# A new order of all steps in a causal-attention and SoLU feed-forward kernel

## The chip, the cores and the metric

One Trainium2 chip, one core of it. The metric is the device time of one execution in microseconds (us); the kernel before was timed three times, and one more execution was profiled. The core has TensorE (PE; its weight loads are PEld), VectorE (DVE), ScalarE (ACT), GpSimd (POOL), and SyncE (SP), which issues most DMA transfers. Each runs its instructions in the order in which they stand in its own queue.

## The reference

Eight batches of eight heads with 576 tokens of 64 numbers each. Four heads see the last 32 positions, four see every 32nd position before them. The attention output of all heads (4,608 tokens of 512 numbers) goes through a feed-forward layer of 1,024 with a SoLU activation and a normalisation.

```python
scores = scale * np.matmul(q, k.transpose(0, 1, 3, 2))
mask_local = (rel >= 0) & (rel < stride)
mask_strided = (rel >= 0) & (pos[None, :] % stride == pos[:, None] % stride)
...
attn = attn / (np.sum(attn, axis=-1, keepdims=True) + 1e-09)
return np.matmul(attn, v).astype(np.float32)
...
h = x @ w_in
h_max = np.max(h, axis=-1, keepdims=True)
e = np.exp(h - h_max)
sm = e / (np.sum(e, axis=-1, keepdims=True) + 1e-09)
solu = h * sm
mu = np.mean(solu, axis=-1, keepdims=True)
var = np.mean((solu - mu) ** 2, axis=-1, keepdims=True)
ln = (solu - mu) / np.sqrt(var + 1e-06) * g_ln
return (ln @ w_out).astype(np.float32)
```

## The kernel before, in words

**Two kinds of work.** Attention is cut into 34 units, each a run of query blocks of one batch and one kind of mask. A unit's steps, in turn: scores and mask on TensorE (L439, its products in L443 and L448), the rows' maximum (L454) and difference (L455) on VectorE, the exponential on ScalarE (L456), the sum (L457) and its reciprocal (L460) on VectorE, the scaling by it on GpSimd (L465), the upper half in 16 bits on ScalarE (L475), the lower half (L479 on VectorE; L477 on GpSimd for the first two batches), a transposing DMA (L481), the output products on TensorE (L487, L505), and a copy of them from PSUM by ScalarE (L543). Queries, keys and values of a batch are loaded by SyncE (L259); values are scaled and split in two 16-bit halves by ScalarE (L400) and VectorE (L401).

The feed-forward layer has 36 tiles of 128 tokens. Ten are plain (L603): two steps of twelve products each. The others go two by two (L646) in seven products of six matrix instructions each (L678, at L681 to L683), which take sums of tokens and of weights in place of some products; GpSimd forms the sums of tokens (L658), ScalarE and VectorE split them in halves (L667, L668), and VectorE joins the products (L706, L710), with a copy by ScalarE (L714). What follows for every tile (L726): the exponential (L746), the product with it (L749), the mean (L752), the centred value's two halves (L753 on ScalarE, L754 on VectorE), the sum of squares (L756), five small steps of GpSimd for the factor of the normalisation (L760 to L764), a transposing DMA (L767), the output product in two halves of twelve matrix instructions (L776, at L771 to L773), and the scaled store (L779). The weights come as 64-bit numbers and are decoded at the start by ScalarE and VectorE (L836 to L838).

**The order.** The function lists 1,598 steps in a `Plan`; a step has an engine, a function that issues its instructions, and the tiles that it reads and writes. Its number is its place of listing. They are issued in the order of the list `ORDER`, written out in the file; `order` only checks that it is complete and that each step stands behind those that it depends on. An engine's queue is thus the steps of that engine, in the order of the list:

```python
def order(self):
    place = {n: i for i, n in enumerate(ORDER)}
    assert sorted(ORDER) == list(range(len(self.steps)))
    assert all(place[d] < place[n] for n, s in enumerate(self.steps) for d in s[2])
    return ORDER
...
for n in plan.order():
    eng = plan.steps[n][0]
    k = len(nc.cur_bb.bb.instructions)
    plan.steps[n][1]()
```

Steps that the texts name by number: 749 and 940 are L754 of two tiles; 786, 788, 793 and 795 join products (L706, L710) and 787, 791, 794, 961, 965 are such products (L678); 628 and 807 are second halves of output products (L776); 848, 867 are scalings of attention units (L465); 1018 is the output product of a unit (L487); 1240, 1252, 1271 and 1292 are scores of four units of one batch (L439), whose output products are 1250, 1262, 1281 and 1302; 1087 to 1151 lie in the products of two pairs.

Of the kernel before, what the change touches and what calls it, by code (L numbers as in the profile page):

```python
# [56 lines left out]
    0, 12, 7, 9, 13, 14, 11, 18, 4, 2, 15, 19, 1, 124, 10, 17, 3, 58, 20, 67, 23, 59, 16, 68, 69, 60, 70, 61, 62, 63, 71, 80, 141, 93, 72, 81, 21, 27, 65, 82,  # L57
    94, 83, 66, 24, 31, 98, 84, 157, 8, 73, 85, 99, 25, 74, 100, 26, 28, 101, 111, 156, 102, 22, 35, 36, 29, 32, 33, 112, 75, 30, 34, 103, 113, 142, 37, 5,
    76, 158, 38, 39, 104, 40, 159, 96, 86, 41, 160, 161, 95, 42, 114, 162, 105, 259, 115, 56, 87, 258, 163, 165, 77, 88, 43, 97, 166, 116, 49, 44, 129, 167,
    57, 106, 293, 164, 168, 78, 89, 54, 266, 130, 169, 117, 45, 118, 267, 170, 268, 79, 47, 279, 131, 64, 292, 171, 46, 119, 125, 90, 143, 269, 50, 280, 52,  # L60
    91, 48, 55, 281, 282, 107, 260, 92, 270, 172, 120, 299, 108, 133, 300, 271, 51, 173, 53, 261, 121, 174, 109, 126, 144, 122, 127, 110, 195, 283, 272, 145,
    301, 132, 137, 262, 128, 325, 284, 175, 194, 134, 123, 146, 135, 294, 312, 147, 176, 138, 136, 295, 273, 274, 148, 196, 177, 197, 326, 313, 198, 210, 139,
    199, 302, 314, 200, 303, 264, 285, 263, 6, 265, 315, 201, 286, 316, 304, 275, 317, 140, 211, 327, 212, 226, 328, 329, 202, 213, 330, 215, 318, 203, 331,
    149, 305, 334, 214, 150, 216, 151, 335, 276, 306, 152, 204, 227, 430, 153, 336, 154, 277, 287, 278, 337, 338, 319, 242, 155, 228, 229, 339, 429, 178, 307,
    288, 308, 298, 180, 231, 297, 217, 289, 340, 296, 230, 290, 320, 179, 341, 232, 206, 181, 347, 233, 437, 220, 438, 342, 321, 291, 218, 439, 243, 309, 184,
    182, 310, 185, 183, 188, 311, 186, 348, 449, 189, 192, 207, 187, 193, 322, 190, 234, 191, 343, 244, 462, 245, 450, 332, 246, 208, 461, 247, 219, 440, 349,
    451, 431, 205, 248, 441, 502, 452, 344, 644, 468, 350, 501, 249, 503, 506, 453, 235, 209, 236, 432, 507, 504, 222, 351, 221, 352, 365, 345, 505, 469, 354,
    508, 510, 250, 353, 223, 442, 454, 511, 509, 252, 355, 512, 253, 470, 443, 251, 356, 366, 323, 346, 238, 471, 513, 436, 224, 514, 324, 367, 455, 368, 463,
    515, 444, 433, 516, 434, 370, 254, 357, 445, 381, 369, 519, 435, 371, 382, 456, 225, 237, 517, 472, 464, 457, 359, 383, 518, 520, 372, 239, 384, 397, 386,
    358, 521, 373, 524, 446, 465, 385, 467, 387, 398, 473, 361, 480, 388, 374, 399, 375, 400, 401, 389, 522, 240, 523, 525, 402, 403, 404, 481, 474, 241, 475,  # L70
    476, 390, 458, 407, 482, 413, 333, 414, 483, 377, 528, 415, 484, 447, 391, 255, 643, 448, 360, 405, 485, 459, 486, 477, 526, 466, 376, 416, 417, 527, 487,
    489, 490, 645, 256, 529, 491, 532, 651, 530, 676, 492, 257, 646, 493, 460, 652, 531, 675, 362, 653, 478, 418, 479, 408, 494, 654, 419, 363, 541, 533, 650,
    663, 655, 534, 542, 537, 538, 495, 649, 364, 406, 549, 656, 378, 535, 496, 657, 664, 539, 497, 543, 540, 420, 553, 536, 544, 550, 665, 545, 546, 551, 648,
    658, 488, 822, 666, 682, 659, 667, 379, 498, 547, 423, 683, 548, 499, 552, 393, 694, 668, 421, 392, 380, 684, 554, 422, 500, 685, 669, 555, 559, 557, 590,
    660, 591, 424, 594, 556, 598, 562, 558, 561, 677, 593, 596, 563, 577, 579, 599, 592, 560, 578, 409, 670, 678, 394, 425, 595, 580, 581, 564, 647, 671, 597,
    565, 695, 604, 582, 602, 583, 606, 686, 584, 600, 566, 395, 687, 567, 568, 601, 603, 605, 607, 608, 612, 569, 679, 571, 688, 570, 609, 615, 614, 616, 396,
    410, 630, 610, 672, 661, 631, 689, 632, 411, 586, 823, 633, 572, 634, 637, 680, 690, 696, 697, 662, 698, 699, 700, 681, 673, 412, 703, 701, 635, 704, 426,
    691, 611, 705, 830, 706, 824, 613, 674, 427, 707, 708, 825, 573, 831, 617, 709, 619, 855, 832, 692, 428, 693, 618, 720, 722, 842, 721, 718, 574, 833, 728,
    854, 715, 620, 710, 716, 636, 834, 717, 719, 621, 723, 843, 844, 827, 575, 724, 1000, 835, 732, 622, 711, 729, 725, 845, 730, 731, 624, 576, 587, 733,
    861, 826, 726, 862, 863, 836, 588, 623, 727, 625, 736, 837, 712, 773, 585, 713, 734, 589, 838, 738, 735, 639, 774, 737, 740, 739, 741, 626, 829, 743, 781,  # L80
    742, 714, 769, 744, 839, 756, 856, 757, 1001, 857, 864, 771, 846, 770, 777, 745, 785, 828, 758, 759, 746, 760, 772, 898, 778, 779, 865, 763, 847, 873,
    627, 761, 860, 747, 783, 848, 762, 782, 780, 849, 628, 850, 784, 748, 874, 750, 787, 786, 866, 867, 791, 629, 851, 775, 638, 899, 749, 788, 793, 794, 795,
    840, 868, 809, 702, 811, 810, 640, 869, 776, 841, 812, 813, 751, 789, 816, 875, 641, 858, 852, 876, 790, 859, 870, 877, 765, 878, 853, 792, 879, 910, 752,
    880, 882, 796, 906, 883, 1033, 814, 797, 871, 872, 884, 815, 894, 1008, 642, 1009, 895, 798, 885, 1010, 753, 1020, 754, 896, 886, 881, 902, 1032, 764,
    1011, 1002, 887, 799, 818, 900, 755, 1012, 903, 1021, 800, 888, 1003, 951, 1013, 817, 1014, 901, 907, 1022, 889, 1023, 908, 897, 766, 801, 1039, 909, 890,
    1233, 767, 904, 1040, 1007, 1015, 905, 912, 952, 891, 1024, 1016, 914, 1041, 803, 911, 892, 768, 1025, 1005, 802, 913, 916, 805, 919, 915, 804, 1026, 959,
    893, 917, 947, 1034, 918, 921, 1042, 920, 1017, 934, 948, 922, 1027, 936, 935, 1028, 1043, 937, 963, 938, 955, 923, 956, 806, 924, 949, 1006, 941, 939,
# [21 lines left out]
    1518, 1536, 1395, 1519, 1396, 1504, 1539, 1407, 1541, 1505, 1520, 1537, 1521, 1408, 1538, 1540, 1508, 1580, 1542, 1544, 1506, 1507, 1549, 1510, 1581,  # L109
    1545, 1523, 1546, 1409, 1509, 1551, 1547, 1548, 1552, 1511, 1550, 1554, 1582, 1512, 1555, 1553, 1567, 1569, 1556, 1568, 1522, 1570, 1557, 1571, 1572,  # L110
    1558, 1573, 1583, 1559, 1560, 1574, 1513, 1584, 1524, 1585, 1586, 1587, 1588, 1576, 1589, 1590, 1525, 1526, 1575, 1561, 1592, 1593, 1577, 1591, 1563,
    1578, 1562, 1564, 1594, 1595, 1565, 1596, 1579, 1566, 1597,
]

BANKED = ("h", "x")
# [881 lines left out]
```

## Time and profile before

| | |
|---|---|
| median of three runs | 556.56 us (555.68 to 556.75) |
| the profiled execution | 555.32 us |
| its span, from the first to the last instruction | 553.4 us |
| granted TensorE clock, mean over the span | 0.969 |
| busy: TensorE, VectorE, ScalarE, GpSimd | 470.8, 419.1, 327.5, 246.7 us |

A share of busy time is a mean over stages with different limits. Idle time of an engine is put down to the instruction whose end released it. TensorE's instructions are pipelined, and their ends are modelled; the granted clock is given as a share of the full 2.4 GHz.

### The profile page before, as it was taken

To read this page: it belongs to the slowest core of one execution; us is meant where nothing else is said; L and a number is where in the kernel's file an instruction comes from. 1 tells how busy PE (TensorE), PEld (TensorE's weight loads), DVE (VectorE), ACT (ScalarE), POOL (GpSimd) and SP (SyncE) were. 2 spreads that over 40 slices of the span, in tenths; PEclk is the share of its full clock that TensorE was granted. 3 is DMA by queue.
4 is the path that set the end of the run, shared out by engine and by line. 5 is a ranking of instruction groups with operands and counts; after the bars stand their busy time and mean duration, and the time that the engine had idled before them with its cause. 6 is when DMAs were issued, how large, how long until landed. Compare 5 with 4: busy or idle time off the path is not lost.

```text
span 553.4 us, 11936 instructions
## 1 busy us (share of the span) xinstructions
PE 470.8 (85%) x4788; PEld 238.6 (43%) x4788; DVE 419.1 (76%) x803; ACT 327.5 (59%) x475; POOL 246.7 (45%) x332
## 2 busy tenths in 40 slices
PE   4378978899989699795899799999889969799996
PEld 3254554434544245342454245343355524344442
DVE  2999879999798947689589965969848985756730
ACT  1997687656865656455466565655666645627440
POOL 3263347998684404423257322647413631462220
PEclk9978999999999999899899999999899999899999
DMA  8999998859969947676596939588766867550471
GB/s 338 372 320 254 271 219 205 166 121 216 254 149 209 224 84 223 96 146 189 111 234 111 191 116 243 134 148 165 214 111 180 146 141 103 100 90 25 101 146 57
DMA packets 168214, 95.78 MB, mean 173 GB/s; under 512 B 138080, under 2 KB 154848, under 8 KB 167648
## 3 DMA queue, kind: packets, MB, share of 16 engines
q1 hardware_dynamic: 162688, 84.84, 69.1%
q10 hardware_dynamic: 5472, 10.20, 6.0%
q8 instruction: 37, 0.61, 0.5%
q14 instruction: 17, 0.14, 0.1%
HBM read 39.24 MB, written 9.44 MB: 88 GB/s over the span
## 4 chain that ended last, share of the span: by engine, by line
DVE 39%; PE 27%; DMA 10%; issue 10%; ACT 9%; POOL 2%; ACTq 0%; SPq 0%; DVEq 0%; POOLq 0%
DVE c L754 5%; DVE eu L749 5%; DMA pt<-p 4%; PE o_ps L771 4%; DVE eu L710 3%; PE o_ps L772 3%; PE o_ps L773 3%; PE h_ps L681 3%; PE h_ps L683 3%; PE h_ps L682 3%; DVE m L457 2%; DVE p L479 2%; DVE m L454 2%; PE x_ps L505 2%; DMA ct<-c 2%
## 5 line engine op out<-in xcount | busy, mean ns | idle before, releaser
L771 PE MATMUL o_ps<-obuf,ct 128*128 128x512 f16 x272 | 105.6, 388 | 9.7 <-ACT ob L779 8.3
L465 POOL TENSOR_TENSOR t<-t,m 128x648 f32<-128x648 f32 (+4 forms) x34 | 55.8, 1644 | 113.8 <-DVE m L462 72.5
L772 PE MATMUL o_ps<-obuf,ct 128*128 128x512 f16 x272 | 104.8, 385 | 0.0
L773 PE MATMUL o_ps<-obuf,ct 128*128 128x512 f16 x272 | 104.6, 385 | 0.0
L658 POOL TENSOR_TENSOR x<-x 128x256 f32<-128x256 f32 x52 | 46.8, 913 | 80.8 <-ACT x L543 79.9
L754 DVE SCALAR_TENSOR_TENSOR c<-eu,st,c 128x1024 f16<-128x1024 f32 x36 | 54.0, 1507 | 11.0 <-ACT c L753 11.0
L753 ACT ACTIVATE c<-eu,st 128x1024 f16<-128x1024 f32 x36 | 41.0, 1143 | 26.5 <-DVE st L752 20.1
L746 ACT ACTIVATE eu<-eu,st,vsc 128x1024 f32<-128x1024 f32 x23 | 28.5, 1237 | 46.8 <-DVE st L736 46.0
L756 ACT ACTIVATE eu<-eu,st 128x1024 bf16<-128x1024 f32 x36 | 41.1, 1142 | 14.5 <-DVE st L752 13.7
L772 PEld LDWEIGHTS <-ct 128*128 128x128 f16 x288 | 28.6, 99 | 40.8 <-issue 11.4
L448 PE MATMUL s_ps<-k,q 64*54 64x54 f32 (+1 forms) x1280 | 41.0, 273 | 3.9 <-DMA q<-qstr 1.6
L771 PEld LDWEIGHTS <-ct 128*128 128x128 f16 x288 | 28.5, 99 | 36.0 <-DMA ct<-c 2.5
L773 PEld LDWEIGHTS <-ct 128*128 128x128 f16 x288 | 28.6, 99 | 35.5 <-issue 2.7
L454 DVE TENSOR_REDUCE m<-s_ps 128x12 f32<-128x648 f32 (+4 forms) x34 | 29.3, 861 | 17.5 <-PE s_ps L448 17.5
L448 PEld LDWEIGHTS s_ps<-k,q 64*54 64x54 f32 (+1 forms) x1280 | 39.9, 199 | 5.0 <-DMA q<-qstr 2.1
L683 PE MATMUL h_ps<-room,obuf 128*128 128x512 f16 x78 | 31.5, 404 | 12.3 <-DVE obuf L668 12.1
L706 DVE TENSOR_TENSOR eu<-eu,h_ps 128x512 f32<-128x512 f32 x39 | 26.7, 683 | 20.2 <-PE h_ps L683 18.4
L681 PE MATMUL h_ps<-room,obuf 128*128 128x512 f16 x78 | 31.4, 403 | 8.3 <-ACT eu L714 5.0
L749 DVE SCALAR_TENSOR_TENSOR eu<-eu,st 128x1024 f32<-128x1024 f32 x26 | 33.3, 1287 | 6.5 <-ACT eu L746 6.4
L779 ACT ACTIVATE ob<-o_ps,st 128x512 f32<-128x512 f32 x34 | 23.0, 677 | 21.4 <-PE o_ps L773 18.8
L456 ACT ACTIVATE t<-t 128x648 f32<-128x648 f32 (+4 forms) x34 | 26.1, 772 | 15.4 <-DVE t L455 14.8
L457 DVE TENSOR_REDUCE m<-t 128x12 f32<-128x648 f32 (+4 forms) x34 | 29.2, 860 | 4.3 <-ACT t L456 4.3
(207 smaller groups left out, 1101.6 us busy)
## 6 DMA issues: line engine op xcount, KB each, us to landing
out<-ob ACTq DMA_DIRECT2D x36, 256.0 KB, 3.4
vtwo<-vstr SPq DMA_DIRECT2D x8, 768.0 KB, 6.8
vd<-vtwo SPq DMA_DIRECT2D x14, 384.0 KB, 5.4
vrl<-vloc SPq DMA_DIRECT2D x8, 640.0 KB, 6.5
k<-kstr SPq DMA_DIRECT2D x8, 594.0 KB, 5.6
k<-kloc SPq DMA_DIRECT2D x8, 576.0 KB, 5.5
q<-qloc SPq DMA_DIRECT2D x8, 576.0 KB, 6.2
q<-qstr SPq DMA_DIRECT2D x7, 594.0 KB, 6.0
```

The lines of the kernel that those rows point to most:

```text
L448: nc.tensor.matmul(s_ps[row : row + nq, pair, i * nk : (i + 1) * nk], q_raw[half][hs, q0 : q0 + (nq - 1) * nqb + 1 : nqb], k_raw[half][hs, ...
L465: add("pool", lambda: nc.gpsimd.tensor_tensor(tv, tv, sm.unsqueeze(2).broadcast_to([P, nx, nk]), op=ALU.mult), r=TM, w=T)
L658: add("pool", lambda: nc.gpsimd.tensor_tensor(s[i], x, y, op=op), r=r, w=SS[i])
L681: nc.tensor.matmul(h_ps[:, bank], hi, w[0][:, c], start=(c == 0), stop=False)
L683: nc.tensor.matmul(h_ps[:, bank], lo, w[0][:, c], start=False, stop=(c == 1))
L749: add("dve", lambda: nc.vector.scalar_tensor_tensor(uv, hv, ia, ev, op0=ALU.mult, op1=ALU.mult, accum_out=us), r=[*HH, E, (ST, "ia")], w=[ ...
L753: add("act", lambda: nc.scalar.activation(c[:, 0], u, AF.Identity, bias=mean, scale=1.0), r=[*U, (ST, "mean")], w=[(C, 0)])
L754: add("dve", lambda: nc.vector.scalar_tensor_tensor(c[:, 1], u, mean, c[:, 0], op0=ALU.add, op1=ALU.subtract), r=[*U, (ST, "mean"), (C, 0) ...
L756: add("act", lambda: nc.scalar.activation(e.bitcast(BF16)[:, 0:DF], u, AF.Square, bias=mean, scale=1.0, accum_out=sq), r=[*U, (ST, "mean") ...
L771: nc.tensor.matmul(o, ct[:, cc, :], ohi[:, cc, :], start=(cc == 0), stop=False)
L772: nc.tensor.matmul(o, ct[:, cc, :], olo[:, cc, :], start=False, stop=False)
L773: nc.tensor.matmul(o, ct[:, 8 + cc, :], ohi[:, cc, :], start=False, stop=(cc == 7))
```

## The change

The list `ORDER` is replaced by another permutation of the same 1,598 numbers, with two-operand steps of VectorE and steps of GpSimd kept apart and idle stretches of TensorE kept short. Nothing else differs. Cut to the lines that hold the first and last steps and those named above:

```diff
--- before.py
+++ after.py
@@ -54,62 +54,62 @@
 
 
 ORDER = [
-    0, 12, 7, 9, 13, 14, 11, 18, 4, 2, 15, 19, 1, 124, 10, 17, 3, 58, 20, 67, 23, 59, 16, 68, 69, 60, 70, 61, 62, 63, 71, 80, 141, 93, 72, 81, 21, 27, 65, 82,
-    94, 83, 66, 24, 31, 98, 84, 157, 8, 73, 85, 99, 25, 74, 100, 26, 28, 101, 111, 156, 102, 22, 35, 36, 29, 32, 33, 112, 75, 30, 34, 103, 113, 142, 37, 5,
...
-    627, 761, 860, 747, 783, 848, 762, 782, 780, 849, 628, 850, 784, 748, 874, 750, 787, 786, 866, 867, 791, 629, 851, 775, 638, 899, 749, 788, 793, 794, 795,
...
-    1035, 961, 1044, 950, 957, 1045, 958, 1004, 925, 1029, 1036, 807, 940, 960, 962, 928, 926, 965, 964, 927, 953, 1038, 966, 969, 808, 1018, 1052, 971, 972,
...
-    1089, 1055, 1031, 1056, 1085, 970, 1057, 1060, 1061, 1049, 1264, 1050, 1130, 1062, 974, 929, 942, 1063, 976, 931, 1075, 1240, 1073, 1064, 1074, 932, 1081,
-    1241, 1076, 1082, 1242, 933, 975, 1265, 1065, 977, 1252, 992, 1083, 1079, 944, 993, 1058, 1131, 1253, 1066, 1080, 996, 1084, 1067, 1068, 1087, 1234, 978,
-    1086, 979, 1243, 995, 1088, 945, 1090, 946, 1254, 1069, 1255, 1235, 1095, 980, 981, 1091, 1128, 983, 1126, 1093, 1092, 1098, 1244, 1097, 1271, 1094, 1099,
...
-    1239, 1259, 1106, 1179, 998, 1180, 1143, 1144, 1184, 1274, 1122, 1145, 1146, 1237, 1148, 1187, 1275, 1181, 1109, 1147, 1276, 1260, 1108, 1151, 1150, 1185,
...
-    1558, 1573, 1583, 1559, 1560, 1574, 1513, 1584, 1524, 1585, 1586, 1587, 1588, 1576, 1589, 1590, 1525, 1526, 1575, 1561, 1592, 1593, 1577, 1591, 1563,
-    1578, 1562, 1564, 1594, 1595, 1565, 1596, 1579, 1566, 1597,
+    14, 58, 9, 18, 15, 7, 11, 19, 59, 31, 23, 124, 60, 12, 17, 13, 10, 1, 61, 62, 63, 0, 93, 141, 142, 67, 16, 4, 94, 27, 65, 66, 68, 20, 21, 32, 24, 69, 70,
+    80, 22, 97, 8, 71, 25, 72, 157, 81, 143, 3, 82, 83, 2, 73, 26, 84, 74, 98, 35, 144, 85, 33, 99, 28, 5, 100, 29, 34, 75, 30, 36, 86, 111, 101, 112, 113,
...
+    858, 747, 627, 847, 780, 748, 750, 784, 625, 863, 749, 864, 786, 787, 788, 628, 859, 848, 791, 629, 794, 765, 840, 865, 866, 640, 793, 898, 795, 809, 810,
+    860, 849, 867, 850, 874, 811, 776, 812, 868, 813, 789, 899, 869, 841, 790, 816, 873, 641, 751, 851, 792, 875, 906, 876, 814, 877, 796, 878, 870, 797, 852,
...
+    920, 917, 947, 805, 1034, 963, 948, 950, 955, 934, 921, 1027, 959, 956, 949, 936, 922, 923, 935, 937, 957, 1028, 768, 938, 939, 924, 1072, 941, 961, 925,
+    940, 1233, 960, 958, 926, 962, 1051, 1035, 927, 1018, 1029, 1037, 964, 1042, 1036, 1077, 928, 1043, 804, 806, 965, 807, 808, 953, 969, 817, 1044, 1052,
...
+    932, 1079, 1076, 1082, 1086, 1087, 1126, 1130, 1264, 1064, 1083, 1084, 942, 933, 1088, 1091, 981, 1080, 944, 1232, 1131, 1093, 979, 1065, 1234, 980, 1090,
+    1066, 1067, 1092, 1095, 1132, 1094, 1068, 945, 1098, 1127, 1096, 1240, 1134, 1100, 1097, 1128, 1235, 1135, 1133, 1069, 1099, 1101, 982, 1070, 1129, 1113,
+    1142, 983, 1102, 1241, 996, 1239, 1115, 1138, 1266, 1242, 1103, 1114, 1252, 1071, 946, 1243, 1116, 1179, 1181, 1104, 984, 1140, 1117, 1180, 1253, 1182,
...
+    1106, 1148, 1411, 1145, 1184, 1147, 1185, 997, 1255, 1151, 1149, 1187, 1153, 1150, 1189, 1238, 1108, 1122, 1410, 998, 1155, 1188, 1154, 1152, 1109, 1256,
+    1166, 1270, 1168, 1121, 1284, 999, 1167, 1257, 1248, 1169, 1191, 1249, 1170, 1156, 1271, 1157, 1258, 1171, 1272, 1172, 1190, 1273, 1193, 1237, 1173, 1269,
...
+    1583, 1572, 1558, 1512, 1582, 1561, 1573, 1584, 1585, 1513, 1524, 1586, 1587, 1525, 1559, 1588, 1560, 1576, 1526, 1575, 1589, 1590, 1563, 1592, 1591,
+    1594, 1577, 1578, 1562, 1564, 1595, 1579, 1593, 1565, 1566, 1596, 1597,
 ]
 
 BANKED = ("h", "x")
```

## Rows read from the trace of the kernel before

**Rows 1.** The page: span, engines' busy time, the chain's shares by engine.

```profile
span 553.4 us, 11936 instructions
...
PE 470.8 (85%) x4788; PEld 238.6 (43%) x4788; DVE 419.1 (76%) x803; ACT 327.5 (59%) x475; POOL 246.7 (45%) x332
...
DVE 39%; PE 27%; DMA 10%; issue 10%; ACT 9%; POOL 2%; ACTq 0%; SPq 0%; DVEq 0%; POOLq 0%
```

**Rows 2.** By stage: us, each engine's busy us (instructions), PEclk, DMA share, GB/s.

```profile
0.00:50.00 50.00, 27.41 (x542) 20.39 (x543) 37.12 (x79) 34.91 (x48) 18.38 (x40) 0.93 1.03 331
50.00:500.00 450.00, 396.17 (x4030) 197.22 (x4030) 359.24 (x681) 270.58 (x397) 216.81 (x269) 0.97 0.77 166
500.00:553.40 53.40, 47.25 (x218) 20.99 (x216) 22.73 (x44) 22.01 (x33) 11.47 (x24) 1.00 0.36 84
```

**Rows 3.** The same, stretches at half clock: first and last of eight.

```profile
51.26:54.68 3.42, 3.42 (x28) 1.41 (x21) 3.00 (x5) 2.99 (x4) 1.41 (x2) 0.50 0.89 204
...
481.34:484.76 3.42, 2.85 (x7) 0.99 (x7) 1.85 (x3) 3.01 (x6) 0.19 (x1) 0.50 0.20 77
```

**Rows 4.** Waits: who waited for whom, us in total, times, longest.

```profile
POOL x L658 <- ACT x L543: 79.9, 10, 14.8
...
PE h_ps L683 <- DVE obuf L668: 12.1, 6, 3.6
```

**Rows 5.** VectorE groups by shape: xcount | busy us, mean ns | idle before.

```profile
L754 DVE SCALAR_TENSOR_TENSOR c<-eu,st,c 128x1024 f16<-128x1024 f32 x36 | 54.0, 1507 | 11.0 <-ACT c L753 11.0
...
L668 DVE TENSOR_TENSOR obuf<-x,obuf 128x512 f16<-128x512 f32 x26 | 21.5, 828 | 2.7 <-ACT obuf L667 2.7
...
L668 DVE TENSOR_TENSOR junk<-x,junk 128x512 f16<-128x512 f32 x13 | 9.2, 709 | 2.7 <-ACT junk L667 2.6
...
L668 DVE TENSOR_TENSOR junk<-x,junk 128x256 f16<-128x256 f32 x13 | 6.0, 465 | 0.0
```

**Rows 6.** L754 and L668 alone: duration ns min/median/max, first and last start, shapes.

```profile
L754 DVE SCALAR_TENSOR_TENSOR c<-eu,st,c x36: 1222/1284/2815, 72.4 to 532.3; 128x1024 f16<-128x1024 f32 x36
...
L668 DVE TENSOR_TENSOR junk<-x,junk x26: 361/654/1027, 154.9 to 496.2; 128x512 f16<-128x512 f32 x13, 128x256 f16<-128x256 f32 x13
L668 DVE TENSOR_TENSOR obuf<-x,obuf x26: 631/682/2082, 163.4 to 505.3; 128x512 f16<-128x512 f32 x26
```

**Rows 7.** Timeline, 259 to 264 us: start, us, engine, line, tiles, idle before.

```profile
259.33 2.05 POOL L465 TENSOR_TENSOR t<-t,m 128x960 f32<-128x960 f32 x1 [4.80 <-DVE m L462]
...
259.65 2.81 DVE L754 SCALAR_TENSOR_TENSOR c<-eu,st,c 128x1024 f16<-128x1024 f32 x1
...
262.60 1.48 DVE L706 TENSOR_TENSOR eu<-eu,h_ps 128x512 f32<-128x512 f32 x2
...
263.35 0.61 PE L681 MATMUL h_ps<-w,obuf 128*128 128x512 f16 x1 [2.97 <-DVE eu L706]
...
263.75 0.63 PE L682 MATMUL h_ps<-w,obuf 128*128 128x512 f16 x1
```

**Rows 8.** Timeline of the start, 10 to 18 us.

```profile
10.57 0.83 DVE L454 TENSOR_REDUCE m<-s_ps 128x12 f32<-128x648 f32 x1 [3.57 <-PE s_ps L448]
...
13.02 1.16 ACT L836 ACTIVATE c<-eu 128x1024 f32<-128x1024 f32 x1 [10.03 <-DMA eu<-w_in]
...
14.72 1.35 ACT L400 ACTIVATE vl<-vrl,vsc 128x1280 f16<-128x1280 f32 x1
```

**Rows 9.** Timeline, TensorE: two units' scores (L443) and outputs (L505).

```profile
359.85 0.40 PE L443 MATMUL s_ps<-mk_loc,unit 64*64 64x480 bf16 x4
...
411.31 0.36 PE L443 MATMUL s_ps<-mk_loc,unit 64*64 64x384 bf16 x4 [0.25 <-DVE vsc L351]
...
412.48 0.28 PE L505 MATMUL x_ps<-pt,ve 96*64 96x64 f16 x6
...
435.12 0.28 PE L505 MATMUL x_ps<-pt,vl 96*64 96x64 f16 x6
```

89 rows, old and new, of the table ORDER are left out of this document.

## The prediction

> **What bounds the kernel now.** I read the page first, then the busy time by stage, then the waits, then the groups by shape, then the timeline at the longest waits. No engine is full: TensorE is busy 470.8 us of 553.4, VectorE 419.1, and the chain that ended last runs 39% on VectorE and 27% on TensorE [rows 1]. So work is handed to and fro between the two, and either one's wait is paid. By stage [rows 2] TensorE stands empty 22.6 us in the first 50 us (loading and decoding), 53.8 us in the 450 us that follow, and 6.2 us in the last 53.4 us, where VectorE has less than half its time to do. What a new order can win lies in the middle 450 us: 53.8 us of TensorE's empty time, and what products lose at half clock. The reader is to see there that GpSimd's long waits, such as 79.9 us for copies of attention output, cost nothing by themselves, while TensorE's waits of 12.1 us for VectorE's `lo` halves (L668) do [rows 4].
>
> Two things in the trace are of the kind that the change is about.
>
> First, **VectorE steps with two operands in SBUF lengthen beside GpSimd**. L754 takes 1222 ns at its shortest and 1284 at the median, but 1507 on average and 2815 at most [rows 5, 6]. At 259.33 GpSimd begins L465; L754 begins 0.32 us later and takes 2.81 us, ending 1.08 us after L465; the two L706 behind it in VectorE's queue start at 262.60, and TensorE waits 2.97 us for them [rows 7].
>
> Second, **half clock**. There are eight stretches after 50 us, each of 3.4 us, in which the granted clock is 0.50 of full, the lower of the two levels (1.2 against 2.4 GHz); the first and the last show TensorE busy 3.42 and 2.85 us of them [rows 3]. The one at 262.9 begins during the wait above, and the two products after it stand 0.40 us apart and take over 0.6 us [rows 7].
>
> **The change, part by part.** No instruction is added or removed: the new list holds the same 1,598 steps. Dependences and buffers are the same. Every cost is thus one of place, on all six in-order queues. Of SyncE's 178 DMA steps 143 stand at another index of its own sequence; but where I add up VectorE's work ahead of each output-product step (both halves, all 36 tiles) in both lists, with the mean time of each shape, the sums differ by under 10 us at each and by near zero on average. The large plan is kept; what changes are exchanges over some microseconds.
>
> *Collisions.* The excess of L754 over its shortest is 36 x (1507 - 1222) ns = 10.3 us; of L668 on `obuf` 26 x (828 - 631) = 5.1 us; of L668 on `junk` 13 x (709 - 631) + 13 x (465 - 361) = 2.4 us [rows 5, 6]. That makes 17.8 us for 88 of the 181 two-operand steps (L754, L668, L749 without PSUM, L479, L401, L838, L856, L891, L813, L616). The other 93 I take at the mean of the `junk` rows, 2.4/26 = 0.09 us: 8.4 us, and 26.2 in all. From the lists in the diff: a GpSimd step stands directly beside 43 of the 181 in the old list and beside 30 in the new; within two places of 65 and 50; within four of 98 and 101. So neighbours are moved apart by a place or two, not further. I take the middle count: 15 fewer of 65, 23%, or 6.0 us of VectorE time. VectorE's share of the chain is 0.39 x 553.4 = 216 us of its 419 busy [rows 1], 52%, so **3.1 us** come off the end. Bounds: nothing (the four-place count), and 6.0 us if all of it is on the chain.
>
> The wait above ends L754 1.08 us after GpSimd's instruction, as if it had hardly run before [rows 7]. The Trainium skill (page "SBUF — State Buffer", section "SBUF: two separate sides") says that of a two-input VectorE instruction and a GpSimd one, whichever starts first holds the shared ports for its whole length and the other is blocked. By that rule a swapped pair only hands the wait to GpSimd, and nothing is saved unless the two are truly apart, which would make the term 0; the row agrees with the rule.
>
> *Half clock.* I went through both lists and added up, between each two TensorE steps, each other engine's work; places where the largest exceeds the first TensorE step's own work by over 3 us are 33 in the old list and 29 in the new, 12% fewer. Of eight stretches that is one. One stretch costs half of its 3.4 us, if products fill it: **1.7 us** [rows 3]. Bounds: none fewer, and four fewer, 6.8 us; two more would cost 3.4.
>
> TensorE in these stretches is busy 2.85 to 3.42 us, so the cost per stretch is real [rows 3]. The Trainium skill ("TensorE: Matmul & The Clock Gate", section "What's actually happening") puts the cost of ramping at under 1% of a span; by that all stretches together would be worth at most 5.5 us, against 13.6 by the rows.
>
> *The longest VectorE stall.* At 260 us the old list has L754 (step 749) directly ahead of the two L706 that TensorE needs, beside the larger L465 (step 867). In the new list 749 is two VectorE steps earlier than L706 step 788, the L465 is gone from beside it, and half an output product (step 628) stands between products 787 and 791. What was 2.97 us should nearly close [rows 7]. I count it within the two terms above, since other places of the new list open, such as between product 961 and step 1018, where the output product 807 that filled it stands later now. What is late next there is VectorE itself.
>
> *The start.* ScalarE waits 10.03 us for `w_in` and begins its first step at 13.02; the splits of `v` (L400, 1.35 us and a longer one) stand behind [rows 8]. The new list puts both ahead of it, into that idle time, as `vr.0` is loaded before `k.1`. VectorE does the two remainders (L401) before the first scores' maximum, which began at 10.57 [rows 8]. So ScalarE may gain up to 2.9 us (twice 1.35 and a little) and VectorE may lose as much. I take zero, and keep 2.9 on both sides. GpSimd now sets `g` squared ahead of its constants; ScalarE needs those only behind the first decode at 13.02 [rows 8], so nothing waits.
>
> *The end.* The last eight output-product halves stand as before and run at clock 1.00 [rows 2]: zero, covered by TensorE itself. The two halves of the last tile's first product change place, but both are needed for its maximum.
>
> *Moved attention units.* Three score steps (1240, 1252, 1271) stand 14 to 26 us of VectorE work later in the new list, and nine products of two pairs (1087 to 1151) 7 to 10 us earlier. The old trace has room: step 1271 runs at 359.85 and its unit's output at 412.48, 52.6 us later, while the next unit needs 23.8 us (411.31 to 435.12) [rows 9]. Cover: that slack. Zero here, and a rival below.
>
> **The sum**: 3.1 + 1.7 = 4.8 us less. The profiled execution took 555.3 us around its span of 553.4 and gives 550.5; the median of the runs is 556.6, 1.2 above that execution, so I forecast **551.8 us**. About 0.2% (1.1 us) is what a measurement of this kernel can tell from no change.
>
> **The rivals.**
> *The collisions only move.* For: within four places the count is the same, and in the old list the steps with a GpSimd neighbour within two places are hardly longer than the others, so the list shows the actual overlap poorly; the longest place of the old list without TensorE work shows no wait in the trace. Every queue is in order, and GpSimd's steps must stand somewhere. Against: the worst pairs, as at 260 us, are visibly taken apart. Time: 556.6, give or take 4.
>
> *The attention units come too late* (slower). With 26.0 us less room, step 1271's unit has 26.6 us from scores to output. From 26.6 us on it decides: the output is then awaited by TensorE's next steps, and by GpSimd's sums (L658), which already wait 79.9 us for such copies [rows 4]. If it takes a third longer than the 23.8 of its neighbour [rows 9], 31.7 us, it is 5.1 us late, and the wait brings one stretch of half clock, 1.7: 6.8 us. With collisions saved as above that is 551.8 + 1.7 + 6.8 = 560.3, without 563.4. For: the unit's ten small steps stand in VectorE's, ScalarE's and GpSimd's queues in turn, each behind whatever is there. Against: 26.6 is still more than 23.8, and the products brought forward make room on VectorE.
>
> **How the numbers follow.** The forecast's case has 0.50, nearly all of it faster. The collisions that only move have 0.27: 0.09 faster, 0.09 same, 0.09 slower. The late units, with other waits of that size, have 0.23. So faster 0.57 (a little of the forecast's case falls within 0.2%), same 0.11, slower 0.32. The range: below, all 6.0 us of collisions on the chain, 6.8 of clock and 2.9 of the start, 540.9; above, the late units, between 560.3 and 563.4. I give 541 to 562; the forecast's own range is 545 to 556.
>
> **What would show it.** Right: L754's mean near 1.40 us or below, L668 on `obuf` below 0.78; seven or fewer stretches at half clock after 50 us; TensorE's empty time in 50 to 500 us down by some 4 us, the middle stage's clock 0.97 or better. Wrong: the same sum of VectorE time with other lines lengthened; GpSimd's L760 to L764 lengthened instead, with their store late; a wait of TensorE for L505's inputs around 385 to 415 us; more than eight stretches at half clock.

## The result and the profile after

The changed kernel takes **511.94 us** (median of four runs, 509.6 to 514.93), the kernel before in the same session 556.65: a ratio of 0.920, 95% interval 0.915 to 0.925. I had forecast 551.8 us and a range of 541 to 562. The direction was right; 44.7 us were gained where I had 4.8.

The page of the kernel after, the lines of [rows 1]:

```profile
span 510.5 us, 11955 instructions
...
PE 463.3 (91%) x4788; PEld 240.0 (47%) x4788; DVE 412.6 (81%) x803; ACT 327.4 (64%) x475; POOL 244.3 (48%) x332
...
PE 40%; DVE 25%; DMA 10%; ACT 9%; issue 7%; POOL 6%; SPq 1%; ACTq 0%; DVEq 0%; POOLq 0%
```

The work is the same (VectorE's busy time shrinks by 6.5 us, TensorE's by 7.5), but the chain that ended last now runs 40% on TensorE, where it ran 39% on VectorE. By stage, the last 53.4 us cut off as in [rows 2]:

```profile
0.00:50.00 50.00, 29.04 (x512) 21.38 (x513) 35.52 (x78) 33.29 (x44) 18.38 (x40) 0.97 1.02 320
50.00:457.10 407.10, 386.41 (x4059) 197.55 (x4059) 352.83 (x676) 270.65 (x396) 215.04 (x267) 0.99 0.89 185
457.10:510.50 53.40, 47.83 (x219) 21.03 (x217) 24.25 (x53) 23.43 (x35) 10.88 (x25) 1.00 0.36 84
```

Start and end are what they were. The middle took 450.0 us and takes 407.1. TensorE's empty time there falls from 53.8 to 407.1 - 386.4 = 20.7 us: 33.1 of the 42.9 us by which the span is shorter. The other 9.8 are busy time, most of it products that no longer run at half clock in this execution. The stretches at half clock behind 50 us, and all that follows the last of them:

```profile
74.60:81.40 6.80, 6.23 (x85) 3.74 (x85) 6.14 (x14) 3.81 (x8) 2.56 (x2) 0.50 1.07 269
183.80:187.20 3.40, 3.40 (x10) 1.20 (x9) 3.40 (x7) 2.30 (x4) 1.81 (x2) 0.50 0.00 0
187.20:510.50 323.30, 310.35 (x2945) 154.63 (x2943) 252.26 (x513) 200.90 (x296) 137.88 (x196) 1.00 0.78 164
```

One of double length and one single, so three of the old length, where there were eight [rows 3]; none from 187 us to the end.

What TensorE's first-layer products (L637, L681, L683) waited for, before in 50 to 500 us (engine, tile, line, for whom: us in total, times, longest), and below it one row of the output products (L771), which wait there for ScalarE's scaled store (L779):

```profile
PE h_ps L683 <- DVE obuf L668: 12.1, 6, 3.6
PE h_ps L637 <- DVE eu L749: 5.3, 5, 2.4
PE h_ps L681 <- ACT eu L714: 5.0, 3, 3.3
PE h_ps L681 <- DVE st L710: 4.4, 7, 1.2
PE h_ps L681 <- DVE eu L706: 4.2, 3, 3.0
PE h_ps L683 <- DVE junk L668: 1.5, 3, 0.8
PE h_ps L681 <- ACT eu L746: 0.5, 1, 0.5
...
PE o_ps L771 <- ACT ob L779: 7.3, 3, 4.1
```

and after, in 50 to 457.1 us:

```profile
PE h_ps L637 <- DVE eu L749: 4.1, 5, 1.8
PE h_ps L683 <- DVE junk L668: 2.4, 1, 2.4
PE h_ps L681 <- DVE eu L706: 1.9, 5, 0.8
PE h_ps L681 <- ACT eu L714: 1.0, 2, 0.8
PE h_ps L681 <- DVE st L710: 0.2, 1, 0.2
...
PE o_ps L771 <- ACT ob L779: 0.2, 1, 0.2
```

The rows of L681 and L683, which are the products of the tiles that go two by two, add up to 27.7 us before and 5.5 after. The 12.1 us for the lower halves on `obuf` are gone. That is 22 of the 33 us of empty time; the wait of the output products for ScalarE's store gives 7.1 more. These are the places in the kernel where most of the gain lies.

VectorE's two-operand steps are shorter, by about what I had forecast [rows 5]:

```profile
L754 DVE SCALAR_TENSOR_TENSOR c<-eu,st,c 128x1024 f16<-128x1024 f32 x36 | 50.0, 1391 | 4.6 <-ACT c L753 4.4
...
L668 DVE TENSOR_TENSOR obuf<-x,obuf 128x512 f16<-128x512 f32 x26 | 18.7, 718 | 0.0
```

So VectorE gave 6.5 us in all and the end moved by 44.7. The experiments ask where the rest comes from.

### The profile page after: what moved, and what is told of

It is laid out like the page before. It is cut to its first block, busy times and chain, and to the rows that moved or that the text cites. A ratio compares the mean times of both kernels' runs of the same rounds, so it can differ in the third digit from the quotient of the medians.

```text
span 510.5 us, 11955 instructions
## 1 busy us (share of the span) xinstructions
PE 463.3 (91%) x4788; PEld 240.0 (47%) x4788; DVE 412.6 (81%) x803; ACT 327.4 (64%) x475; POOL 244.3 (48%) x332
## 4 chain that ended last, share of the span: by engine, by line
PE 40%; DVE 25%; DMA 10%; ACT 9%; issue 7%; POOL 6%; SPq 1%; ACTq 0%; DVEq 0%; POOLq 0%
PE o_ps L771 6%; PE o_ps L773 6%; PE o_ps L772 6%; DMA ct<-c 4%; PE h_ps L681 4%; PE h_ps L683 4%; PE h_ps L682 4%; DVE c L754 3%; DMA vrl<-vloc 3%; DMA pt<-p 3%; PE x_ps L505 3%; DVE eu L749 2%; PE s_ps L448 2%; DVE m L454 2%; DVE m L457 2%
## 5 line engine op out<-in xcount | busy, mean ns | idle before, releaser
L771 PE MATMUL o_ps<-obuf,ct 128*128 128x512 f16 x272 | 104.0, 383 | 4.0 <-DMA ct<-c 2.9
L773 PE MATMUL o_ps<-obuf,ct 128*128 128x512 f16 x272 | 103.8, 382 | 0.0
L772 PE MATMUL o_ps<-obuf,ct 128*128 128x512 f16 x272 | 103.6, 381 | 0.0
L465 POOL TENSOR_TENSOR t<-t,m 128x648 f32<-128x648 f32 (+4 forms) x34 | 51.9, 1528 | 90.7 <-DVE m L462 77.4
L658 POOL TENSOR_TENSOR x<-x 128x256 f32<-128x256 f32 x52 | 42.4, 831 | 65.4 <-ACT x L543 64.3
L754 DVE SCALAR_TENSOR_TENSOR c<-eu,st,c 128x1024 f16<-128x1024 f32 x36 | 50.0, 1391 | 4.6 <-ACT c L753 4.4
L771 PEld LDWEIGHTS <-ct 128*128 128x128 f16 x288 | 28.2, 98 | 37.4 <-DMA ct<-c 5.0
L746 ACT ACTIVATE eu<-eu,st,vsc 128x1024 f32<-128x1024 f32 x23 | 28.5, 1240 | 24.6 <-DVE st L736 24.4
L749 DVE SCALAR_TENSOR_TENSOR eu<-eu,st 128x1024 f32<-128x1024 f32 x26 | 35.1, 1349 | 5.1 <-ACT eu L746 4.6
L475 ACT CAST p<-t 128x648 f16<-128x648 f32 (+4 forms) x34 | 25.6, 759 | 14.6 <-POOL t L465 13.8
L779 ACT ACTIVATE ob<-o_ps,st 128x512 f32<-128x512 f32 x34 | 23.2, 683 | 17.8 <-PE o_ps L773 11.4
L762 POOL TENSOR_SCALAR st<-st 128x1 f32<-128x1 f32 x36 | 20.8, 577 | 24.5 <-ACT eu L756 21.2
L681 PE MATMUL h_ps<-room,obuf 128*128 128x512 f16 x78 | 29.7, 380 | 1.3 <-ACT eu L714 1.2
```

The lines of the kernel that those rows point to most:

```text
L465: add("pool", lambda: nc.gpsimd.tensor_tensor(tv, tv, sm.unsqueeze(2).broadcast_to([P, nx, nk]), op=ALU.mult), r=TM, w=T)
L658: add("pool", lambda: nc.gpsimd.tensor_tensor(s[i], x, y, op=op), r=r, w=SS[i])
L681: nc.tensor.matmul(h_ps[:, bank], hi, w[0][:, c], start=(c == 0), stop=False)
L749: add("dve", lambda: nc.vector.scalar_tensor_tensor(uv, hv, ia, ev, op0=ALU.mult, op1=ALU.mult, accum_out=us), r=[*HH, E, (ST, "ia")], w=[ ...
L754: add("dve", lambda: nc.vector.scalar_tensor_tensor(c[:, 1], u, mean, c[:, 0], op0=ALU.add, op1=ALU.subtract), r=[*U, (ST, "mean"), (C, 0) ...
L771: nc.tensor.matmul(o, ct[:, cc, :], ohi[:, cc, :], start=(cc == 0), stop=False)
```

## The experiments

In their texts the old or base list is that of the kernel before. In kernels with a longer list or an added function the line numbers are higher (L684 for L681, L671 for L668; with the fills L699 for L683, L684 for L668, L752 for L736).

**Without the collisions.** In both kernels GpSimd's three tensor-by-tensor steps (L465, L477, L658) keep their place but read one column only and fill their tile twice, so that they last about as long and hardly read. GpSimd's other steps, which also read, stay as they are, so most collisions go, not all. What the filled steps leave out is the scaling of the attention weights, the first two batches' lower halves and the sums of tokens.

```diff
-            add("pool", lambda: nc.gpsimd.tensor_tensor(s[i], x, y, op=op), r=r, w=SS[i])
+            def sum_filled():
+                nc.gpsimd.tensor_tensor(s[i][:, :, 0:1], x[:, :, 0:1], y[:, :, 0:1], op=op)
+                for _ in range(2):
+                    nc.gpsimd.memset(s[i], 0.01)
+
+            add("pool", sum_filled, r=r, w=SS[i])
```

The old list:

> The old order. GpSimd's large two-operand steps (L465, L477, L658) are replaced by a one-column step of the same kind and two memsets of the whole output, about as long, which read nothing in SBUF; the results are therefore not the reference's. Collisions theory (the 43 us were VectorE steps held up by GpSimd's reads, multiplied by TensorE waits and half clock): near the new kernel, 510 to 525 us. Placement theory (the new order lets TensorE's waits run beside other work; collisions are 5 us of it): 545 to 556 us.

The new list:

> The new order, with the same replacement of GpSimd's large steps. Both theories: a little below the new kernel's 512, 500 to 512 us. The distance to the old order with the same replacement is what placement alone is worth: under 15 us by the collisions theory, over 30 us by the placement theory.

Measured: 538.44 us for the old list (0.967 of the kernel before, 0.958 to 0.976) and 511.17 for the new one (0.918, 0.907 to 0.929). Page of the old list's kernel, then of the new one's:

```profile
PE 466.4 (87%) x4788; PEld 237.5 (44%) x4788; DVE 395.3 (74%) x803; ACT 327.1 (61%) x475; POOL 251.0 (47%) x524
```

```profile
PE 463.0 (91%) x4788; PEld 241.2 (48%) x4788; DVE 394.7 (78%) x803; ACT 325.6 (64%) x475; POOL 252.8 (50%) x524
```

VectorE loses 23.8 us of work in the one and 17.9 in the other, and GpSimd is no less busy. The old list turns this into 18.2 us, the new one into 0.8, against the medians of the result (the intervals of the two times with the fills are 5 and 6 us to each side, so the 0.8 can't be told from nothing). The collisions are still in the new list; they cost it next to nothing. And with most of them gone the lists are still 27.3 us apart. Neither theory's numbers came: 538 lies between the two ranges for the old list, and 27.3 between "under 15" and "over 30". In the old list's kernel, with no step moved, the row of L683 with `obuf` falls from 12.1 us to this:

```profile
PE h_ps L699 <- DVE obuf L684: 5.4, 6, 1.8
```

**Mixtures.** All steps sorted by their place in one list in blocks of 40, and within a block by the other list.

```diff
-sorted(range(1598), key=lambda n: old_place[n])
+sorted(range(1598), key=lambda n: (old_place[n] // 40, new_place[n]))
```

> Blocks of 40 steps of the old list, each sorted within by the new list. If the gain lies in the exchanges of neighbours within some 13 us (as the change's words say): 512 to 530 us. If it lies in where work stands over more than that (attention units moved by 14 to 26 us, products brought forward): 540 to 556 us.

> The mirror image: blocks of 40 steps of the new list, each sorted within by the old list. Gain among neighbours: 535 to 556 us. Gain in the large placement: 512 to 525 us.

Measured: 607.75 us (1.091, 1.077 to 1.106) and, the lists exchanged, 637.95 (1.146, 1.134 to 1.157). The cores view of the second:

```profile
core 0: 634.8 us, clock 0.919
```

Both are far worse than either list and outside all four ranges, so they don't say which scale carries the gain. Probably the cuts at 40 places tear apart what belongs together in both; that was not tried. With two levels, a mean of 0.919 means 16% of the span at half clock.

**Twelve of TensorE's steps.** In the old list, 12 of 277, at places where the trace shows a wait. Three of the moves:

```diff
-808, 1018, 1052
+926, 1018, 965
...
-1170, 1193, 1171
+1111, 1193, 1283
...
-1163, 1430, 1307
+1164, 1430, 1312
```

> The old list with only 12 of TensorE's 277 steps moved, each one or two steps earlier or later in TensorE's own queue, at places where the trace of before shows it waiting for a step that was not ready; all other queues keep the old sequence. Theory A (the time of the old list is lost at TensorE's waits, one by one, and each is cured where it stands): about 11 us of waiting goes, 546 us, between 541 and 551. Theory B (a wait that is taken away at TensorE comes back at the next one, because VectorE's work sets the pace): 554 to 558 us.

Measured: 545.39 us, 0.981 (0.977 to 0.985). Theory A, to the microsecond. The row of L683 with `obuf` falls from 12.1 to 5.2, while that of L681 with ScalarE's copy (L714) rises from 5.0 to 7.7:

```profile
PE h_ps L686 <- DVE obuf L671: 5.2, 4, 2.4
```

The control, 12 others drawn by lot (194, 210, 1217 and nine more):

```diff
-175, 194, 134
+312, 194, 147
...
-1331, 1217, 1347
+1373, 1217, 1427
```

> A control for the 12 TensorE moves: 12 other TensorE steps, drawn by lot among those that may be moved, by the same one or two steps in TensorE's queue. Theory A (a move gains where the trace shows TensorE waiting): nothing gained, 556 to 566 us. If any loosening of the list gains: 545 to 552 us.

Measured: 563.0 us, 1.012 (1.009 to 1.016). Moves drawn by lot gained nothing: this one draw cost 7.2 us (against 555.8 in its session), where those at the waits gained 10.6.

**Many moves of all engines, SyncE's and GpSimd's too.** One kernel from the old list, one from the new, chosen for TensorE's waits with the durations held as the traces show them. The texts speak of 285 and 148 single moves, but the lists of the two kernels hold more: within the engines' own queues it takes at least 627 single moves to get from the old list to the first, 84 of them of SyncE's transfers, and at least 587 from the new list to the second, 81 of them of SyncE's. So both are new orders of the whole, and not a few moves. A stretch of the second:

```diff
-1167, 1257, 1248, 1169, 1191, 1249, 1170, 1156, 1271
+1167, 1169, 1170, 1237, 1259, 1272, 1260, 1247, 1173
```

> The old list with 285 single steps of all engines moved, one at a time, each by at most some 80 places, so that TensorE's steps come up when their inputs are ready by the durations that the trace of before and the trace of after show; the list stays nearer to the old one (mean displacement 12 places) than to the new one (15). Theory A (what counts is that each step of TensorE finds its inputs ready; many lists do that, and the new one is only one of them): most of the gain or more, under 520 us, about 500. Theory C (the large placing of the new list is needed): at 535 us or above. Theory D (every list that is not kept whole falls apart, as the two mixtures did): above 560 us.

> The new list with 148 single steps moved in the same manner. Theory A: the waits that the new list has left at TensorE (44.6 us between its steps) shrink by half, 497 us, between 487 and 506. Theory D: slower than the new list, above 520 us. If the order is not what holds the new list back any more: 508 to 515 us.

Measured: 557.81 us (1.004, 1.002 to 1.006) and 545.63 (0.980, 0.977 to 0.983), the latter 33.7 us slower than the list it came from. A miss twice. By stage, the first 50 us of the one from the old list and of the one from the new list:

```profile
0.00:50.00 50.00, 17.11 (x315) 14.12 (x315) 28.75 (x58) 24.27 (x30) 16.89 (x37) 1.00 0.82 293
```

```profile
0.00:50.00 50.00, 22.20 (x473) 17.36 (x473) 32.96 (x66) 26.10 (x32) 18.41 (x39) 0.93 0.95 329
```

TensorE loses 10 and 7 us of work there against 27.4 and 29.0. Over the whole span VectorE's busy time is up from 419.1 to 428.3 and from 412.6 to 421.2 us. A choice that holds all durations fixed sees neither late loads nor collisions that come back; which of the two, or what else, made these kernels slow was not tried.

**The loads alone.** The old list with SyncE's 178 transfers in the sequence of the new one, all other queues old. The first eight:

```diff
-14, 11, 18, 15, 19, 17, 23, 16
+14, 18, 15, 11, 19, 31, 23, 17
```

> The old list for TensorE, VectorE, ScalarE and GpSimd, and SyncE's queue alone, 178 transfers, in the sequence of the new list. Theory E (the new sequence of loads brings a good part of the gain): 525 to 545 us. Theory A: the sequence of loads fits the list that it was made with; alone it gains nothing, and transfers that the old list wants early stand behind ones that it wants late: 560 to 585 us.

Measured: 607.21 us, 1.092 (1.087 to 1.096). TensorE's longest waits are now for transfers:

```profile
PE s_ps L451 <- DMA k<-kloc: 15.6, 3, 8.1
PE o_ps L774 <- DMA ct<-c: 15.0, 5, 4.6
PE x_ps L508 <- DMA pt<-p: 9.4, 2, 6.9
```

Before, the first of these rows is absent and the other two stand at 1.4 and 3.5 us. So the new sequence of loads brings nothing by itself and costs 51 us without its list. A transfer that the old list needs early stands behind others that wait: the copies of the split values in SyncE's queue (L417, here L420) wait 37.0 us for VectorE's remainders on `vl` (L401), where it was 7.2. It is a part of the new order that must fit. A changed sequence of loads probably also hurt the mixtures and the two kernels above; that was not tried by itself.

**Where along the span.** One list up to a place, the other from there. Up to place 530, and up to 1060, the two lists hold the same steps but for nine, and up to any other place looked at (each 50 from 100 on) but for 16 at most, so a seam disturbs little.

```diff
-sorted(range(1598), key=lambda n: old_place[n])
+sorted(range(1598), key=lambda n: min(old_place[n], 530) + max(new_place[n], 530))
```

> The first 530 places of the old list, then the steps that are left in the sequence of the new one. The two lists hold nearly the same steps by that place, and the trace of after reaches the same TensorE work there some 3 us later than that of before. Theory A (the gain is a sum of what single stretches save, and a stretch carries no condition over to the next): 509 us, between 505 and 515, so no slower than the new list. Theory D (the list works as a whole only): above 525 us.

> The first 1060 of the 1598 places of the new list, then the rest in the sequence of the old one. The trace of after reaches that place 22 us earlier than that of before. Theory A: 534 us, between 529 and 540. Theory D: at the time of the old list or above, 555 us and more.

> The mirror: the first 1060 places of the old list, then the rest in the sequence of the new one. Theory A: the new list saves some 20 us behind that place, so 536 us, between 530 and 541; this and the run before it then save 44 us together, what the whole change saves. Theory D: 555 us and more. A seam that costs something by itself shows as a sum of both savings under 44 us.

Measured: 509.35 us (0.916, 0.913 to 0.919), 532.88 (0.960, 0.954 to 0.966) and 539.36 (0.970, 0.966 to 0.974). The traces, cut at the end of the last TensorE step ahead of places 530 and 1060, before and after:

```profile
0.00:160.20 160.20, 127.34 (x1675) 72.94 (x1676) 136.41 (x251) 113.64 (x160) 93.78 (x119) 0.97 0.94 244
160.20:344.90 184.70, 158.01 (x1635) 77.71 (x1633) 141.07 (x268) 102.86 (x151) 70.71 (x96) 0.96 0.77 166
344.90:553.40 208.50, 185.47 (x1481) 87.95 (x1479) 141.61 (x286) 110.99 (x165) 82.18 (x118) 0.97 0.60 125
```

```profile
0.00:162.50 162.50, 131.82 (x1714) 76.36 (x1715) 136.63 (x252) 110.95 (x156) 84.77 (x110) 0.97 0.99 238
162.50:321.50 159.00, 150.55 (x1550) 76.30 (x1549) 135.81 (x274) 107.65 (x159) 79.48 (x106) 0.99 0.91 194
321.50:510.50 189.00, 180.92 (x1527) 87.31 (x1525) 140.16 (x278) 108.77 (x160) 80.06 (x117) 1.00 0.66 139
```

The three stretches change by +2.3, -25.7 and -19.5 us. Taking the old list for the first gains 2.6 against the new kernel; against the old kernel's 557.12 in the same session the new list saves 24.2 up to 1060 and 17.8 from there on. The saving is thus a sum of stretches: 42.0 of 44.7, and the 2.7 us that are left for the seams lie within the intervals. Until 160 us, with VectorE busy 136 of them in both, the order hardly mattered; it did where VectorE has room (141 of 184.7 us) and TensorE still waited. That VectorE's room is the reason was not tried.

**Nine moves in the new list.** TensorE's queue alone; two of them:

```diff
-600, 602, 599
+395, 602, 582
...
-334, 276, 335
+306, 276, 334
```

> The new list with 9 of TensorE's steps moved by one to three steps in TensorE's queue alone, where the trace of after still shows it waiting; loads and all other queues keep the new sequence. Theory A: some 5 to 7 us of waiting goes, 505 to 508 us. Theory B (the waits come back one step on): 510 to 514 us. Theory D (the new list stands no disturbance, as the 148 moves showed): above 516 us.

Measured: 508.69 us (0.915, 0.911 to 0.918), 3.3 us off the new kernel's median: between theories A and B. The intervals of the two overlap (the new list's is 0.915 to 0.925), so how much of the waiting came back is not settled.

**Moves and collisions together.** The 12 TensorE moves with GpSimd's fills (the two edits shown above, no others):

> The old list with the 12 moves of TensorE's steps, and GpSimd's tensor-by-tensor steps replaced by fills as in the first experiment (results are not the reference's). Alone, the fills gave 538.4 us and the moves 545.4 us, where the kernel before took about 556.6. If collisions and misplaced steps are two causes that add: 528 us, between 524 and 531. If they are the same waits, lengthened once by the collision and once by the place: 534 to 539 us.

Measured: 531.97 us (0.956, 0.952 to 0.961), between the two cases: the moves are worth 6.4 us without most collisions (538.4 - 532.0) and 10.6 with them.

**Thirty moves, VectorE's above all.** In the old list; loads and GpSimd's sequence untouched. One of VectorE's:

```diff
-1155, 1182, 1156, 1121, 1168, 1157, 1188, 1195
+1155, 1182, 1188, 1156, 1121, 1168, 1157, 1195
```

> The old list with 30 single steps moved by one to eight places in the queue of their own engine: 17 of VectorE, 8 of TensorE, 5 of ScalarE. SyncE's loads and GpSimd's steps keep the old sequence. The moves were chosen so that the steps that TensorE waits for in the trace of before come up earlier on VectorE and ScalarE. By adding up what the trace's waits give back, 25 us: 532 us. Theory A' (a few steps at the wrong place on VectorE make most of the 27 us that are left without collisions): 526 to 538 us. Theory B (VectorE's work sets the pace, what one step gains its neighbour loses): 545 to 556 us.

Measured: 531.91 us, 0.955 (0.951 to 0.958); forecast 532. Over half of the change's gain, with 30 of 1,598 steps moved by one to eight places. The move shown, in the timelines. Before (start, us, engine, line, operation, tiles, idle before):

```profile
389.96 0.38 PE L682 MATMUL h_ps<-room,obuf 128*128 128x512 f16 x1
390.51 1.29 DVE L749 SCALAR_TENSOR_TENSOR eu<-eu,st 128x1024 f32<-128x1024 f32 x1 [0.90 <-ACT eu L746]
...
391.91 0.68 DVE L668 TENSOR_TENSOR obuf<-x,obuf 128x512 f16<-128x512 f32 x1
...
392.65 0.61 PE L683 MATMUL h_ps<-room,obuf 128*128 128x512 f16 x1 [2.31 <-DVE obuf L668]
```

and with the moves:

```profile
373.62 0.68 DVE L671 TENSOR_TENSOR obuf<-x,obuf 128x512 f16<-128x512 f32 x1
...
374.36 0.39 PE L686 MATMUL h_ps<-room,obuf 128*128 128x512 f16 x1
...
374.61 1.28 DVE L752 SCALAR_TENSOR_TENSOR eu<-eu,st 128x1024 f32<-128x1024 f32 x1 [0.31 <-ACT eu L749]
```

The lower half that L683 needs is 0.68 us of work, its median [rows 6]. Its upper half was ready since 382.7 us and VectorE idle for 0.90 us, but its queue held L749 first, which waited for ScalarE. TensorE waited 2.31 us, and the product behind the wait takes 0.61 us instead of 0.38: one of the eight stretches at half clock begins here. Moved ahead, the half is ready, the wait is gone and so is the slow product.

A collision has a part in it even so, further up. ScalarE was late because L736, a VectorE step on three columns that lasts 0.16 us at the median, ran beside GpSimd's L465 and took 1.71:

```profile
387.30 1.79 POOL L465 TENSOR_TENSOR t<-t,m 128x960 f32<-128x960 f32 x1
387.39 1.71 DVE L736 TENSOR_TENSOR st<-st,vsc 128x3 f32<-128x3 f32 x1
389.14 1.24 ACT L746 ACTIVATE eu<-eu,st,vsc 128x1024 f32<-128x1024 f32 x1 [5.54 <-DVE st L736]
```

The same step with the moves, and then, from the old list with the fills, the same step and TensorE's wait behind it:

```profile
371.49 1.72 DVE L739 TENSOR_TENSOR st<-st,vsc 128x3 f32<-128x3 f32 x1
```

```profile
374.16 0.16 DVE L752 TENSOR_TENSOR st<-st,vsc 128x3 f32<-128x3 f32 x1
...
377.86 0.39 PE L699 MATMUL h_ps<-room,obuf 128*128 128x512 f16 x1 [0.76 <-DVE obuf L684]
```

So one wait goes in two ways. Without the collision it falls from 2.31 us to 0.76; with the step moved it is gone although the collision is still there.

With the fills:

> The old list with the 30 single moves, and GpSimd's tensor-by-tensor steps replaced by fills (results are not the reference's). The moves alone gave 531.9 us, the fills alone 538.4. If placing and collisions are two costs that add: 531.9 - 18.2 = 514 us, about the new list's time (between 510 and 518). If the moves have already taken the waits through which the collisions cost time, as in the new list: 525 to 532 us. The 12 TensorE moves showed a middle case (6.4 us of their 10.6 left without collisions): by that, 519 to 524.

Measured: 520.42 us, 0.934 (0.930 to 0.938): the middle case. With the runs above this makes a table of medians (the first row's and the last one's "as it is" from the session of the result; TensorE empty is span less busy time):

| list | as it is | GpSimd's reads gone | worth of the collisions | TensorE empty, as it is |
|---|---|---|---|---|
| before | 556.7 us | 538.4 us | 18.2 us | 82.6 us |
| 12 moves | 545.4 | 532.0 | 13.4 | 74.4 |
| 30 moves | 531.9 | 520.4 | 11.5 | 65.3 |
| after | 511.9 | 511.2 | 0.8 | 47.2 |

Each worth carries the intervals of its two times, some 3 to 7 us, so the two rows in the middle can't be told apart. From the first to the last it is clear: the less TensorE stands empty in a list, the less its collisions cost.

**On top of the best list** (old to 530, then new): 11 moves of TensorE's steps, and in another kernel 24 of VectorE's, ScalarE's and TensorE's. Two of the first, one of the second:

```diff
-674, 692, 613
+703, 692, 617
...
-600, 602, 599
+395, 602, 582
```

```diff
-1150, 1189, 1238
+1155, 1189, 1188
```

> The first 530 places of the old list and the rest of the new one (509.35 us), with 11 TensorE steps moved by one or two steps in TensorE's queue. Theory A: 5 us less, 503 to 506 us. Theory B: 508 to 511 us.

> The same list with 24 steps moved by one to eight places in the queue of their own engine: 14 of VectorE, 6 of ScalarE, 4 of TensorE. Theory A: 10 us less, 497 to 502 us. If collisions that the list had avoided come back with the moves of VectorE's steps, as VectorE's busy time would show (above 415 us): 505 us or more.

Measured: 507.97 us (0.913, 0.909 to 0.916) and 511.21 (0.918, 0.912 to 0.924). Of the 5 and 10 us that the waits seemed to hold, 1.4, which the intervals don't tell from nothing, and nothing came. In the second VectorE is busy 417.0 us where the list had 412.0, which speaks for collisions that came back with the moves. The first has the lowest median of the study. None of its runs (507.36 to 508.88) is as slow as the fastest of the changed kernel (509.6), though the sessions differ.

## Why the prediction was wrong

**The collisions.** VectorE's saving was right: 6.0 us forecast, 7.3 found on the 181 steps counted and 6.5 on all of VectorE, L754 and L668 on `obuf` below the bounds that I set. The whole excess was near too, 26.2 us estimated and 23.8 gone with the fills, though some 4 of these are L736 (from 9.8 to 5.7 us), which the 181 leave out. By the exclusive lock that the Trainium skill states ("SBUF — State Buffer", "SBUF: two separate sides"), exchanged pairs would only hand the wait to GpSimd. But GpSimd's busy time also fell, from 246.7 to 244.3 us, so here steps did come apart. Failed is the step "VectorE's share of the chain is ... 52%", used as a rate of exchange. In the old list 23.8 us of VectorE's time are worth 18.2 us, 76%; in the new one 17.9 are worth 0.8, 4%. What a microsecond of VectorE is worth depends on whether TensorE comes to wait for it, as the wait at 392.65 shows, and the new list changed this also for the collisions that are still there: that is 17.4 us (18.2 - 0.8) of its gain. I priced only those taken away.

**TensorE's waits.** This is the large failure, in two sentences: "what changes are exchanges over some microseconds", and of the stall at 260 us "I count it within the two terms above, since other places of the new list open". The first is true, since up to any place looked at the lists hold the same steps but for 16 at most; that it makes the change small was wrong. 27.3 us separate the lists with most collisions gone, and 30 exchanges over one to eight places make 24.6 with the collisions and 18.0 (538.4 - 520.4) without. The stall itself was not one place: it is a kind, the products L681 and L683 waiting, 27.7 us in sum, 22.2 of them for VectorE and 5.5 for ScalarE. In three of the six waits for a lower half on `obuf` the half itself is lengthened beside L465 (2.08, 1.76 and 1.21 us); in the other three it lasts 0.68 us and stands behind longer steps. Each cure takes its part of the 12.1 us: 5.4 are left with GpSimd's reads gone, 5.2 with the 12 moves, 1.1 with the 30, nothing in the new list. I showed this row [rows 4] as what matters, and then gave its removal no term. That new places would open was argued from the list, with nothing weighed against it; the rows that grew, L683 with `junk` (1.5 to 2.4 us) and the transposed tiles (4.0 to 7.0), make 3.9 us.

**Half clock.** In the two profiled executions five stretches fewer, not one. Counting places in the list where another engine's work exceeds TensorE's by 3 us (33 to 29) did not find what the trace shows: each of the eight stretches begins in or within 1.3 us behind a wait of TensorE of 2.1 to 4.1 us, as at 392.65, and most of those waits went. The price was mis-sized as well, 1.7 us a stretch. In the experiments' sessions the kernel before ran 37 times, at mean granted clocks from 0.951 to 0.975. Its five runs at 0.954 have a median of 557.75 us, the five at 0.975 one of 555.04: by the two levels 23 us more at half clock, about seven stretches, for 2.7 us, an estimate of 0.4 us a stretch. And the changed kernel's run at 0.975 took 514.93 us, where the five of the kernel before at that clock took 554.4 to 556.5. So at the same clock the lists are some 40 us apart, and the clock carries little of the gain.

**The start and the end.** Zero for each was near enough. The first 530 places cost 2.3 us more, as the trace and the kernel that takes them from the old list (2.6) agree, inside the 2.9 that I kept. The end is the same 53.4 us.

**The rivals.** Neither came. The moved units made no wait: TensorE's longest for L505 in the middle is 1.7 us, for a transposed tile. That the collisions only move is near the truth in one respect: GpSimd's five small steps L760 to L764 take 102.3 us where they took 94.4, L761 639 ns on average where it took 431. But the stores behind them are not late: the row of L771 with L779 went from 7.3 to 0.2 us.

```profile
L761 POOL TENSOR_SCALAR st<-st,vsc 128x1 f32<-128x1 f32 x32 | 20.4, 639 | 3.2
```

**The signs.** Each of those for right came: L754 at 1391 ns, `obuf` at 718, three stretches, a middle clock of 0.99. Of those for wrong, half of one came, the longer L760 to L764. Set just beyond a sum of 4.8 us, the signs could not tell it from nine times as much; TensorE's empty time, down 33 us where I named 4, could.

What stays open: the 20 us that lie between the 30 moves and the new list were not taken apart further. The range of 541 to 562 was built from the same terms, so it could not hold 512 either.

## What to carry to other kernels

Where two engines hand work to and fro and neither is full, price a new order from the bounding engine's waits: add up, by kind, what it waits for, and look at what stands ahead of each awaited step in its own engine's queue. A short step moved ahead of a long one that is itself waiting cost VectorE nothing here (its idle time ahead of L749 fell from 0.90 to 0.31 us). The trace of the old list named such places well enough that 30 moves brought what was forecast, to the microsecond. In the list that was already good it did not: of 5 and 10 us, 1.4 and nothing came. Make few moves at a time, leave the queue of transfers alone, and look after each round whether VectorE's busy time has risen.

## What was not expected of the hardware

What collisions cost the kernel is no property of the collisions: about 18 to 24 us of VectorE's time went with GpSimd's reads in each list, and the end moved by 0.8 us in one and 18.2 in the other. The size of a step does not protect it: L736 works on three columns and lasted 1.71 us beside L465 where its median is 0.16. And one queue of transfers, with the same 178 transfers in a sequence made for another list, costs 51 us, more than the whole change brought.
